# Keeping an input weight by head pairs on 128 rows in an attention-and-MLP kernel

## The chip, the cores and the metric

The kernel runs on one core of a Trainium2 chip. The number that counts is the device time of one execution in microseconds (us), taken as the median of several runs. Times inside an execution come from one profiled execution; its instructions are grouped by source line, and "L399" is line 399 of the kernel as it was before the change.

## What is computed

For each of 8 batches and 8 heads there is a block `x` of 512 tokens by 64 and a block `state` of 32 tokens by 64. Both attend to each other, and the result (512 + 32 tokens, 8 x 64 = 512 wide) goes through a two-layer network with a Mish activation:

```
scores = x @ state.T / 8 ;  xread = softmax(scores) @ state          # (512, 64) per head
scores2 = state @ x.T / 8 ; sread = softmax(scores2) @ x             # (32, 64) per head
y = [xread, sread] with the heads side by side                       # (8 * 544, 512)
h = y @ w_in ; g = h * tanh(log(1 + exp(h))) ; out = g @ w_out       # w_in (512, 2048), w_out (2048, 512)
```

`x` and `state` are 32-bit floats; `w_in` and `w_out` come as 64-bit floats, 8 MB each.

## The kernel before, in words

**The product with the state.** The 512 read tokens of a batch are never formed. Since `xread @ w_in` is softmax times (`state @ w_in`), the kernel first makes the small product `state @ w_in` for a slice of columns (`sw_slice`, PSUM tiles `swp`), splits it into a rounded part and a remainder (`swh`, `swl`), and multiplies that by the transposed softmax (`aT`, split into `ah` and `al`): this is `gemm1`, three products of 128x512 per pair. ScalarE applies Mish (`take_g`), VectorE splits the result (`gh`, `gl`), and `gemm2` multiplies by `w_out`, which is kept in split form too (`wo`).

**Slots.** A slot is one batch `b` and one of eight pieces `j`: 256 of the 2048 columns of `w_in`, that is 12 matmuls of `gemm1` and 24 of `gemm2`. From batch 1 on, one `sw_slice` serves two slots; in batch 0 each slot has its own, half as wide. Four more slots (`gemm1_s`) do the 256 `sread` tokens; before batch 7 they are put in. The slots run one after the other, `gemm2` two slots behind.

**Halves of heads.** Before the change the eight heads are used as two groups, heads 0 to 3 and heads 4 to 7. `w_in_sb` holds 64 rows per head twice: rows 0 to 63 the lower half of the 2048 columns, rows 64 to 127 the upper half, all eight heads beside each other. The state product is 16 matmuls with 64 contraction rows and 32 output rows: for each of two groups, four heads, two halves of the columns. The compiled program issues each as two instructions. For the `sread` slots this layout has to be regrouped: `load_w_s` copies pieces of `w_in_sb` inside SBUF by DMA, 16 transfers of 256 KB.

**Loads.** In batch 0 the weights arrive while the work on them has begun. `load_w_in(e)` brings piece e of `w_in` (called i0 to i7 below) as two transfers, each to 64 rows, in runs of 1 KB; `load_w_out(j)` brings two blocks of 128 rows of `w_out` (o0 to o7) in runs of 4 KB. A raw piece is two 32-bit words per number. ScalarE rescales the high words (`scale_high`, L101) and rounds the low words (`round_low`, L108; for most `w_out` pieces GpSimd does it, L106), and VectorE joins them into a 32-bit float (`join_words`, L119). For `w_out`, VectorE then splits into `wo` (L156, L159). All these loads, and `x`, go through SyncE's queue in the order in which they are written; the first batch's state goes through ScalarE's queue, as three transfers of 32 KB. i0, i1 and i4 to i7 share two buffers, so i4 can start only when i0 is joined. i2 and i3 lie in the places that o6 and o5 take later, and o7 takes the place of the first batch's `x`.

**Order.** Every engine runs its own instructions in order. A scheduler places them; `with behind(...)` in the code says after which earlier instruction something may stand in that order. `fill` issues matmuls whose results nobody uses, between the steps of the first batch.

Of the kernel before, what the change touches and what calls it, by code (L numbers as in the profile page):

```python
# [16 lines left out]
P = 128  # L17
# [22 lines left out]
def state_attention_mish_kernel(ctx, tc, x, state, w_in, w_out, out):  # L40
# [20 lines left out]
    w_in_sb = const.tile([P, H, DF // 2], F32, name="w_in_sb")  # L61
# [6 lines left out]
    def load_x(b):  # L68

        shape = [P, NC, 2, NT * D]  # L70
        if b == 0:
            xs = const.tile(shape, F32, tag="wo7", name="x_0")
        else:
            xs = pool.tile(shape, F32, tag="x", name=f"x_{b}", bufs=1)
        for c in range(NC):
            last["load"] = nc.sync.dma_start(
                xs[:, c], x[b].rearrange("(k c) (p t) d -> c p k (t d)", k=2, t=NT)[c])
        return xs
# [6 lines left out]
    def load_xq(b, xq, parts):  # L85
        for i in parts:
            h, q = divmod(i, 4)
            u, dh = divmod(q, 2)
            nc.sync.dma_start(
                xq[q * 32:(q + 1) * 32, h % NC, h // NC],  # L90
                x[b, h].rearrange("(i w u) d -> u i w d", w=8, u=2)[u][:, :, dh * 32:(dh + 1) * 32])
# [30 lines left out]
    def load_w_in(e):  # L122


        shape, place = [P, H, P, 2], {2: "wo6", 3: "wo5"}.get(e)
        if place:
            raw = const.tile(shape, U32, tag=place, name=f"wir_{e}")
        else:
            raw = pool.tile(shape, U32, tag="raw", name=f"wir_{e}", bufs=2)
        for r in range(2):  # L130
            f0 = 2 * (r * DF // 2 + e * P)
            last["load"] = nc.sync.dma_start(  # L132
                raw[half(r)].rearrange("p c f w -> p c (f w)"),
                w_in[:, f0:f0 + 2 * P].rearrange("(h d) f -> d h f", d=D),
            )
# [63 lines left out]
    def attention(b, xs, sn, xq=None):  # L199
# [97 lines left out]
        def soft1_e():  # L297
# [11 lines left out]
            for kc in two:  # L309
                mx = small["mx"][kc]  # L310
                with behind(*(((0, "sub"),) if b == 0 and kc else ())):
                    nc.vector.tensor_reduce(mx, groups(src[kc]), AX.X, ALU.max)
                last[b, "sub"] = nc.vector.tensor_sub(groups(e1[kc]), groups(src[kc]), wide(mx))
                last[b, "exp"] = nc.scalar.activation(e1[kc], e1[kc], AF.Exp)
# [52 lines left out]
        if b == 0:  # L367
            first = [lambda: (xt(0), xt(1), state_blocks(b, sn), xt(2), xt(3), s_(), soft1_e()),
                     soft1_n, soft1_a]
# [22 lines left out]
    def sw_slice(b, j, n=2 * P):  # L392

        pw = [misc(f"swp_{b}_{j}_{r}") for r in range(2)]
        for kc in range(2):
            for c in range(NC):
                o = slice(c * NS, (c + 1) * NS)
                for r in range(2):
                    last["PE"] = nc.tensor.matmul(  # L399
                        pw[r][o, kc * n:(kc + 1) * n],  # L400
                        bds[b][half(r), kc ^ r, o],
                        w_in_sb[half(r), kc * NC + c, j * P:j * P + n],
                        start=True, stop=True,
                    )
        hi = pool.tile([P, 2, 2, n], F32R, tag="swh", name=f"swh_{b}_{j}")
        lo = pool.tile([P, 2, 2, n], F32R, tag="swl", name=f"swl_{b}_{j}")
        for r in range(2):
            hr = hi[:, r].rearrange("p k f -> p (k f)")
            pr = pw[r][:, :2 * n]
            last["swh"] = nc.scalar.copy(hr, pr)  # L410
            last["swl"] = nc.vector.tensor_sub(lo[:, r].rearrange("p k f -> p (k f)"), pr, as_f32(hr))  # L411
        return {j + i: [t[..., i * P:(i + 1) * P] for t in (hi, lo)] for i in range(n // P)}
# [16 lines left out]
    def gemm1(b, j, aT, sw):  # L429
        swh, swl = sw[j]  # L430
        phs = []
        for k in range(2):
            ph = ps_h.tile([P, 512], F32, tag="ph", name=f"ph_{b}_{j}_{k}")
            seq = []
            for kc in range(2):
                hi, lo = aT[kc]
                seq += [(swh[:, k, kc], hi), (swh[:, k, kc], lo), (swl[:, k, kc], hi)]
# [13 lines left out]

    def load_w_s(j):
        w = pool.tile([P, NC, 2, 2 * P], F32, tag="raw", name=f"ws_{j}", bufs=2)
        f0 = 2 * j * P
        for kc in range(2):
            for r in range(2):
# [4 lines left out]
    def gemm1_s(j, ws):  # L461
# [3 lines left out]
        for r in range(2):  # L465
            for k in range(2):
                w = ws[:, :, r, k * P:(k + 1) * P]
# [17 lines left out]
    def gemm2(key, fcs, gh, gl, ntok, ts=None):  # L485
# [3 lines left out]
        for t in ts or range(ntok):  # L489
            for i, fc in enumerate(fcs):  # L490
# [3 lines left out]
                for n, (g, w) in enumerate(ops):  # L494
                    last["PE"] = nc.tensor.matmul(  # L495
                        accs[key][t], g[:, sl], wo[fc % 8][:, fc // 8, w, :],
# [31 lines left out]
    load(("o", 4), ("i", 6), ("o", 5), ("i", 7), ("o", 6), ("o", 7))  # L528

    first[0]()  # L530
    with behind((0, "exp")):
        scale_words(raws[0])
    new_accs(0, NT)
# [6 lines left out]
    first[1]()  # L540
    with behind("words"):
        scale_high(rawo[0])
    with behind((0, "e1")):
        join_w_in(0, raws.pop(0))
    with behind("PE", "words", "join"):
        first[2]()
    fill(1)
    with behind((0, "ah")):
        round_low(rawo[0])
    with behind("PE", "words", (0, "DVE")):  # L550
        sw_next = sw_slice(0, 0, P)
    fill(2)
    with behind("swh"):
        round_low(raws[1], True)
        scale_high(raws[1])
    ws = {}
    with behind("swl"):
        ws[0] = join_w_out(0, rawo.pop(0))
    with behind("join"):
        join_w_in(1, raws.pop(1))  # L560
# [30 lines left out]
    for n, (key, j) in enumerate(slots):  # L591
        if key == "s":
            if j == 0:
                ws_next = load_w_s(0)
            ws, ws_next = ws_next, load_w_s(j + 1) if j + 1 < 4 else None
            g = gemm1_s(j, ws)
            pending.append((key, (2 * j, 2 * j + 1, 2 * j + 8, 2 * j + 9), g, 2))
# [8 lines left out]
        if (key, j) == (0, 0):  # L606
            with behind("words"):
                g = mish(key, j, phs)
            with behind("PE", "mish"):
                sw_next = sw_slice(0, 1, P)  # L610
# [9 lines left out]
        pending.append((key, (j, j + 8), g, NT))  # L620
        if key == 0 and j + 1 < SLOTS:
# [79 lines left out]
```

## Time and profile before

| | before |
|---|---|
| median of 3 runs | 693.2 us (693.12 to 695.12) |
| profiled execution | 700.21 us, of which 698.4 us from the first to the last instruction |
| TensorE matmul (PE) busy | 682.4 us, 98% |
| VectorE (DVE) / ScalarE (ACT) busy | 342.6 us / 263.6 us |
| mean granted TensorE clock | 0.986 of full speed |
| read from HBM | 32.24 MB, at 219 to 228 GB/s until about 87 us |
| `w_in` transfers | 16 of 512 KB, median 18.4 us from issue to landing |
| `w_out` transfers | 16 of 512 KB, median 13.7 us |

In the views below, a row of the timeline is: start, length, engine, line, operation, what it writes and reads, how many, and in brackets how long the engine sat idle before it and what ended that. A matmul's end is modelled by the profiler; the starts are measured.

### The profile page before, as it was taken

How to read it: one execution, taken by the hardware profiler on the slowest of the kernel's cores; microseconds unless marked ns; L12 is line 12 of the kernel's file. 1: busy time of each engine (PE TensorE's matmuls, PEld its weight loads, DVE VectorE, ACT ScalarE, POOL GpSimd, SP SyncE). 2: the span in 40 equal slices, each digit the busy share in tenths (PEclk: the TensorE clock that was granted, in tenths of full speed). 3: DMA queues.
4: the chain of work that ended last, by engine and by line, in shares of the span. 5: the costliest groups of instructions: out<-in, count | busy, mean ns of one | idle time of the engine just before them, and what ended most of it. 6: DMA issues, size and time to landing. Idle time of an engine off the chain costs nothing.

```text
span 698.4 us, 11183 instructions
## 1 busy us (share of the span) xinstructions
PE 682.4 (98%) x4718; PEld 529.9 (76%) x4718; DVE 342.6 (49%) x520; ACT 263.6 (38%) x416; POOL 10.6 (2%) x14
## 2 busy tenths in 40 slices
PE   7989999999999999999999999999999999999997
PEld 6767677677777777777777777777777788977785
DVE  2876598484338433753357333843374334332221
ACT  2887666362226312451146122631255113222110
POOL 0001200000000000000000000000000000000000
PEclk8989999999999999999999999999999999999999
DMA  9999832410123010312032011334010007001001
GB/s 224 221 219 228 226 49 68 103 22 23 42 68 49 9 61 20 85 25 61 6 82 41 28 34 66 49 69 121 16 46 1 1 1 181 1 0 31 1 1 61
DMA packets 84530, 46.09 MB, mean 66 GB/s; under 512 B 57600, under 2 KB 78080, under 8 KB 84480
## 3 DMA queue, kind: packets, MB, share of 16 engines
q1 hardware_dynamic: 84048, 45.27, 27.4%
q8 instruction: 37, 0.61, 0.4%
q10 hardware_dynamic: 432, 0.10, 0.1%
q14 instruction: 13, 0.11, 0.1%
HBM read 32.24 MB, written 8.91 MB: 59 GB/s over the span
## 4 chain that ended last, share of the span: by engine, by line
PE 91%; DMA 3%; SPq 2%; ACT 2%; DVE 1%; issue 0%; ACTq 0%; DVEq 0%
PE acc L495 52%; PE ph L441 24%; PE swp L399 5%; PE ph_s L473 3%; PE acc_s L495 3%; DMA wor<-in_moe_w_out_dram 2%; PE srp L348 1%; PE sc L230 1%; SPq L132 1%; PE e2p L276 1%; DMA x<-in_x_dram 1%; SPq L146 1%; ACT L416 1%; ACT g L416 0%; DMA out_dram<-o 0%
## 5 line engine op out<-in xcount | busy, mean ns | idle before, releaser
L495 PE MATMUL acc<-wo,gh 128*128 128x512 f32 x1024 | 329.3, 403 | 0.0
L495 PEld LDWEIGHTS acc<-wo,gh 128*128 128x128 f32 x1024 | 190.3, 190 | 55.6 <-issue 12.3
L495 PE MATMUL acc<-wo,gl 128*128 128x512 f32 x512 | 202.5, 397 | 0.0
L416 ACT ACTIVATE g<-ph 128x512 f32<-128x512 f32 x128 | 74.1, 597 | 221.8 <-DVE gl L423 154.6
L421 DVE CAST gh<-g 128x1024 fp32r<-128x1024 f32 x64 | 44.3, 693 | 161.5 <-PE acc L495 145.9
L495 PEld LDWEIGHTS acc<-wo,gl 128*128 128x128 f32 x512 | 97.2, 190 | 23.6 <-DVE swl L411 0.4
L441 PE MATMUL ph<-ah,swh 128*128 128x512 f32 x256 | 84.2, 401 | 1.9 <-ACT swh L410 1.9
L423 DVE TENSOR_TENSOR gl<-g,gh 128x1024 fp32r<-128x1024 f32 x64 | 78.4, 1226 | 4.9
L441 PE MATMUL ph<-al,swh 128*128 128x512 f32 x256 | 79.5, 392 | 0.0
L441 PE MATMUL ph<-ah,swl 128*128 128x512 f32 x256 | 79.0, 392 | 0.2 <-DVE swl L411 0.2
L411 DVE TENSOR_TENSOR swl<-swp,swh 128x512 fp32r<-128x512 f32 (+1 forms) x72 | 42.7, 625 | 54.4 <-ACT swh L410 53.9
L441 PEld LDWEIGHTS ph<-ah,swh 128*128 128x128 f32 x256 | 47.3, 188 | 15.2 <-ACT swh L410 2.9
L441 PEld LDWEIGHTS ph<-ah,swl 128*128 128x128 f32 x256 | 47.8, 188 | 11.1 <-DVE swl L411 0.6
L441 PEld LDWEIGHTS ph<-al,swh 128*128 128x128 f32 x256 | 48.1, 188 | 10.7
L399 PE MATMUL swp<-w_in_sb,bd 64*32 64x256 f32 (+1 forms) x1152 | 41.1, 364 | 3.8 <-DVE w_in_sb L119 3.7
L410 ACT CAST swh<-swp 128x512 fp32r<-128x512 f32 (+1 forms) x72 | 35.6, 546 | 18.2 <-PE swp L399 18.2
L416 ACT ACT_TABLE_LOAD x21 | 26.9, 1283 | 28.0 <-PE e2p L276 11.3
L399 PEld LDWEIGHTS swp<-w_in_sb,bd 64*32 64x32 f32 x1152 | 18.8, 108 | 21.8 <-issue 14.3
L504 ACT COPY o<-acc 128x512 f32<-128x512 f32 x16 | 9.4, 587 | 44.9 <-PE acc L495 25.1
L470 DVE TENSOR_TENSOR wl<-ws,wh 128x512 fp32r<-128x512 f32 x16 | 11.1, 691 | 27.3 <-PE ph_s L473 23.3
L208 DVE STREAM_TRANSPOSE xT<-xq 128x512 f32<-128x512 f32 x24 | 24.2, 1087 | 0.3 <-PE e2p L276 0.3
L502 DVE COPY o<-acc 128x512 f32<-128x512 f32 x16 | 11.0, 690 | 22.4 <-DMA out_dram<-o 16.4
(83 smaller groups left out, 523.7 us busy)
## 6 DMA issues: line engine op xcount, KB each, us to landing
x<-in_x_dram SPq DMA_DIRECT2D x32, 256.0 KB, 4.2
wir<-in_moe_w_in_dram SPq DMA_DIRECT2D x16, 512.0 KB, 18.4
wor<-in_moe_w_out_dram SPq DMA_DIRECT2D x16, 512.0 KB, 13.7
out_dram<-o SPq DMA_DIRECT2D x32, 256.0 KB, 2.3
xq<-in_x_dram SPq DMA_DIRECT2D x192, 32.0 KB, 2.3
ws<-w_in_sb SPq DMA_DIRECT2D x16, 256.0 KB, 4.7
sn<-in_state_dram SPq DMA_DIRECT2D x21, 32.0 KB, 1.8
out_dram<-o_s SPq DMA_DIRECT2D x8, 64.0 KB, 1.7
```

The lines of the kernel that those rows point to most:

```text
L208: nc.vector.transpose(xTs[c].rearrange("p (k v i g) -> p g k v i", k=2, v=2, g=4), xq[:, c].rearrange("p k (g v) d -> p g k v d", v=2))
L399: last["PE"] = nc.tensor.matmul(pw[r][o, kc * n:(kc + 1) * n], bds[b][half(r), kc ^ r, o], w_in_sb[half(r), kc * NC + c, j * P:j * P + n], ...
L410: last["swh"] = nc.scalar.copy(hr, pr)
L411: last["swl"] = nc.vector.tensor_sub(lo[:, r].rearrange("p k f -> p (k f)"), pr, as_f32(hr))
L416: last["mish"] = nc.scalar.activation(g[:, k * 512:(k + 1) * 512], ph, AF.Mish)
L421: nc.vector.tensor_copy(gh, g)
L423: last["gl"] = nc.vector.tensor_sub(gl, g, as_f32(gh))
L441: last["PE"] = nc.tensor.matmul(ph, l, r, start=(i == 0), stop=(i == len(seq) - 1))
L470: nc.vector.tensor_sub(lo, w, as_f32(hi))
L473: nc.tensor.matmul(ph[r][:, k * 256:(k + 1) * 256], l[:, c], srT[i][:, c], start=(c == 0 and n == 0), stop=(c == NC - 1 and n == 2))
L495: last["PE"] = nc.tensor.matmul(accs[key][t], g[:, sl], wo[fc % 8][:, fc // 8, w, :], start=(fc == 0 and n == 0), stop=(fc == NFC - 1 and ...
L502: nc.vector.tensor_copy(o, accs[key][t])
```

## The change

The heads are now used as even and odd ones. `w_in_sb` holds 128 rows of `w_in` (two neighbouring heads) on 128 partitions, four pairs beside each other, with all 2048 columns in their natural order. A piece of `w_in` is loaded as two transfers of two pairs each, to all 128 rows, in runs of 2 KB. The state product becomes 8 matmuls: for each of four pairs, the even head on rows 0 to 63 and the odd one on rows 64 to 127, each over twice as many columns (512; 256 in batch 0). The `sread` slots read `w_in_sb` as it is, and `load_w_s` is gone. `x` and `state` are put in the new order when they are loaded; for the state this gives the source four blocks of 32 rows with gaps between them, where it was 128 rows on end. Piece j of `w_out` is now the blocks 2j and 2j+1, not j and j+8. In batch 0 the words of i0 and i1 are rescaled earlier, those of o0 later, and the last loads stand in another order.

```
-    w_in_sb = const.tile([P, H, DF // 2], F32, name="w_in_sb")
+    w_in_sb = const.tile([P, NC, DF], F32, name="w_in_sb")
...
     def load_w_in(e):
-        shape, place = [P, H, P, 2], {2: "wo6", 3: "wo5"}.get(e)
+        shape, place = [P, NC, 2 * P, 2], {2: "wo6", 3: "wo5"}.get(e)
...
-        for r in range(2):
-            f0 = 2 * (r * DF // 2 + e * P)
+        w = w_in.rearrange("(c p) f -> p c f", p=P)[..., 4 * e * P:4 * (e + 1) * P]
+        for c in range(0, NC, 2):
             last["load"] = nc.sync.dma_start(
-                raw[half(r)].rearrange("p c f w -> p c (f w)"),
-                w_in[:, f0:f0 + 2 * P].rearrange("(h d) f -> d h f", d=D),
-            )
+                raw[:, c:c + 2].rearrange("p c f w -> p c (f w)"), w[:, c:c + 2])
...
     def load_state(b):
             (nc.sync if b else nc.scalar).dma_start(
-                sn[:, i, :], state[b].rearrange("(a c) n d -> a (c n) d", a=2)[i % 2])
+                sn[:, i, :], state[b].rearrange("(c a) n d -> a c n d", a=2)[i % 2])
...
-    def sw_slice(b, j, n=2 * P):
-        pw = [misc(f"swp_{b}_{j}_{r}") for r in range(2)]
+    def sw_slice(b, j, n=2):
+        f = slice(j * 2 * P, (j + n) * 2 * P)
+        pw = [misc(f"swp_{b}_{j}_{kc}")[:, :n * 2 * P] for kc in range(2)]
+        for c in range(NC):
+            o = slice(c * NS, (c + 1) * NS)
+            for kc in range(2):
+                last["PE"] = nc.tensor.matmul(
+                    pw[kc][o, :], bds[b][half(kc), 0, o], w_in_sb[half(kc), c, f], start=True, stop=True)
...
-    def load_w_s(j):
-        w = pool.tile([P, NC, 2, 2 * P], F32, tag="raw", name=f"ws_{j}", bufs=2)
-        f0 = 2 * j * P
-        for kc in range(2):
-            for r in range(2):
-                nc.sync.dma_start(
-                    w[half(kc), :, r], w_in_sb[half(r), kc * NC:(kc + 1) * NC, f0:f0 + 2 * P])
-        return w
...
-    load(("o", 4), ("i", 6), ("o", 5), ("i", 7), ("o", 6), ("o", 7))
+    load(("o", 4), ("o", 6), ("o", 5), ("i", 6), ("i", 7), ("o", 7))
...
-    with behind((0, "exp")):
+    with behind((0, "scs")):
         scale_words(raws[0])
...
+    with behind((0, "exp")):
+        scale_words(raws[1])
...
+    with behind("swh", "join"):
+        scale_words(rawo[0])
         ws[0] = join_w_out(0, rawo.pop(0))
```

Three places in the compiled order. The first is ScalarE in batch 0, from the first exponentials (L314, `e`) to the first Mish. The tiles `wir_96` and `wir_102` are i0 and i1, `wor_99` is o0, and `wir_105` is i2. Before:

```order
L314 ACTIVATE e_0_0_207<-e_0_0_207 128x512
L314 ACTIVATE e_0_1_208<-e_0_1_208 128x512
L101 ACTIVATE wir_96<-wir_96 128x1024
L108 ACTIVATE wir_96<-wir_96 128x1024
L101 ACTIVATE wor_99<-wor_99 128x1024
L334 CAST ah_0_272<-at_0_267 128x512
L334 CAST ah_1_281<-at_1_276 128x512
L108 ACTIVATE wor_99<-wor_99 128x1024
L410 CAST swh_0_306<-swp_0_0_288 128x256
L410 CAST swh_0_306<-swp_0_1_289 128x256
L101 ACTIVATE wir_102<-wir_102 128x1024
L416 ACT_TABLE_LOAD
```

And now:

```order
L101 ACTIVATE wir_96<-wir_96 128x1024
L108 ACTIVATE wir_96<-wir_96 128x1024
L313 ACTIVATE e_0_0_209<-e_0_0_209 128x512
L313 ACTIVATE e_0_1_210<-e_0_1_210 128x512
L101 ACTIVATE wir_102<-wir_102 128x1024
L108 ACTIVATE wir_102<-wir_102 128x1024
L333 CAST ah_0_273<-at_0_268 128x512
L333 CAST ah_1_282<-at_1_277 128x512
L403 CAST swh_0_298<-swp_0_0_288 128x256
L403 CAST swh_0_298<-swp_0_1_289 128x256
L101 ACTIVATE wor_99<-wor_99 128x1024
L108 ACTIVATE wor_99<-wor_99 128x1024
```

Both words of i0 now stand before the exponentials and both of i1 before `ah`; the words of o0 have moved behind `swh`.

The second place is SyncE's queue after the load of the second batch's `x` (`x_126`). Before, `wir_138` and `wir_144` were i6 and i7, and `wor_135`, `wor_141`, `wor_147`, `wor_150` were o4 to o7:

```order
L76 DMA x_126<-in_x_dram 128x2x256 x4
L165 DMA sn_131<-in_state_dram 128x64 x3
L146 DMA wor_135<-in_moe_w_out_dram 128x1024 x2
L165 DMA sn_1143<-in_state_dram 128x64 x3
L132 DMA wir_138<-in_moe_w_in_dram 64x8x256 x2
L146 DMA wor_141<-in_moe_w_out_dram 128x1024 x2
L132 DMA wir_144<-in_moe_w_in_dram 64x8x256 x2
L146 DMA wor_147<-in_moe_w_out_dram 128x1024 x2
```

Now `wor_138` is o6, `wor_141` is o5, and `wir_144` and `wir_147` are i6 and i7:

```order
L76 DMA x_126<-in_x_dram 128x2x256 x4
L163 DMA sn_131<-in_state_dram 128x1x64 x3
L144 DMA wor_135<-in_moe_w_out_dram 128x1024 x2
L163 DMA sn_1071<-in_state_dram 128x1x64 x3
L144 DMA wor_138<-in_moe_w_out_dram 128x1024 x2
L144 DMA wor_141<-in_moe_w_out_dram 128x1024 x2
L132 DMA wir_144<-in_moe_w_in_dram 128x2x512 x2
L132 DMA wir_147<-in_moe_w_in_dram 128x2x512 x2
```

The two `w_out` pieces stand ahead of the two `w_in` pieces; a transfer of `w_in` has 128 rows with two runs of 512 words, where it had 64 rows with eight runs of 256.

The third place is TensorE around the state product of slot 4 in batch 0. Before:

```order
L441 MATMUL ph_3_1_575<-ah_1_281,swl_3_511 128x512
L399 MATMUL swp_4_0_585<-w_in_sb,bd_167 32x128 x8
L399 MATMUL swp_4_1_586<-w_in_sb,bd_167 32x128 x8
L495 MATMUL acc_0_233<-wo_449,gh_2_516 128x512 x2
L495 MATMUL acc_0_233<-wo_449,gl_2_517 128x512
```

And now:

```order
L435 MATMUL ph_3_1_543<-ah_1_282,swl_3_479 128x512
L398 MATMUL swp_4_0_553<-w_in_sb,bd_167 32x256 x4
L398 MATMUL swp_4_1_554<-w_in_sb,bd_167 32x256 x4
L480 MATMUL acc_0_233<-wo_425,gh_2_484 128x512 x2
L480 MATMUL acc_0_233<-wo_425,gl_2_485 128x512
```

The slice stands at the same place; it has half as many matmuls, each over twice the columns.

More of the change, by code (lines that the diff above doesn't have):

```diff
@@ L313, in soft1_e @@
                 last[b, "sub"] = nc.vector.tensor_sub(groups(e1[kc]), groups(src[kc]), wide(mx))
-                last[b, "exp"] = nc.scalar.activation(e1[kc], e1[kc], AF.Exp)
+                with behind(*(("words",) if b == 0 else ())):
+                    last[b, "exp"] = nc.scalar.activation(e1[kc], e1[kc], AF.Exp)
         def soft1_n():
@@ L367, in attention @@
         if b == 0:
-            first = [lambda: (xt(0), xt(1), state_blocks(b, sn), xt(2), xt(3), s_(), soft1_e()),
-                     soft1_n, soft1_a]
+            first = [lambda: (xt(0), xt(1), state_blocks(b, sn), xt(2), xt(3), s_()),
+                     soft1_e, soft1_n, soft1_a]
             fills.append(fill)
@@ L389, in attention @@
         return [], pieces, aT
-    def sw_slice(b, j, n=2 * P):
-        pw = [misc(f"swp_{b}_{j}_{r}") for r in range(2)]
-        for kc in range(2):
-            for c in range(NC):
-                o = slice(c * NS, (c + 1) * NS)
-                for r in range(2):
[L399 to L412, printed above, removed]
+    def sw_slice(b, j, n=2):
[6 more added lines that the diff above has]
+                    pw[kc][o, :], bds[b][half(kc), 0, o], w_in_sb[half(kc), c, f], start=True, stop=True)
+        hi = pool.tile([P, 2, n * 2 * P], F32R, tag="swh", name=f"swh_{b}_{j}")
+        lo = pool.tile([P, 2, n * 2 * P], F32R, tag="swl", name=f"swl_{b}_{j}")
+        for kc in range(2):
+            last["swh"] = nc.scalar.copy(hi[:, kc], pw[kc])
+            last["swl"] = nc.vector.tensor_sub(lo[:, kc], pw[kc], as_f32(hi[:, kc]))
+        return {j + i: [t[:, :, i * 2 * P:(i + 1) * 2 * P] for t in (hi, lo)] for i in range(n)}
     def take_g(g, k, ph):
@@ L436, in gemm1 @@
                 hi, lo = aT[kc]
-                seq += [(swh[:, k, kc], hi), (swh[:, k, kc], lo), (swl[:, k, kc], hi)]
+                h, l = (t[:, kc, k * P:(k + 1) * P] for t in (swh, swl))
+                seq += [(h, hi), (h, lo), (l, hi)]
             seq = seq[::3] + seq[1::3] + seq[2::3]
@@ L449, in mish, with gemm1_s @@
         return g
-    def load_w_s(j):
-        w = pool.tile([P, NC, 2, 2 * P], F32, tag="raw", name=f"ws_{j}", bufs=2)
-        f0 = 2 * j * P
-        for kc in range(2):
-            for r in range(2):
-                nc.sync.dma_start(
-                    w[half(kc), :, r], w_in_sb[half(r), kc * NC:(kc + 1) * NC, f0:f0 + 2 * P])
-        return w
-    def gemm1_s(j, ws):
+    def gemm1_s(j):
         g = new_g(f"s_{j}")
@@ L466, in gemm1_s @@
             for k in range(2):
-                w = ws[:, :, r, k * P:(k + 1) * P]
+                fc = 4 * j + 2 * r + k
+                w = w_in_sb[:, :, fc * P:(fc + 1) * P]
                 hi, lo = (pool.tile([P, NC, P], F32R, tag="t", name=f"w{n}_{j}_{r}_{k}", bufs=5) for n in "hl")
@@ L539, in state_attention_mish_kernel @@
     fill(0)
-    first[1]()
-    with behind("words"):
-        scale_high(rawo[0])
+    first[2]()
+    with behind((0, "exp")):
+        scale_words(raws[1])
     with behind((0, "e1")):
@@ L545, in state_attention_mish_kernel @@
     with behind("PE", "words", "join"):
-        first[2]()
+        first[3]()
     fill(1)
[L548 to L551, printed above, removed]
+    with behind("PE", (0, "ah"), (0, "DVE")):
+        sw_next = sw_slice(0, 0, 1)
     fill(2)
-    with behind("swh"):
-        round_low(raws[1], True)
-        scale_high(raws[1])
     ws = {}
     with behind("swl"):
+        join_w_in(1, raws.pop(1))
+    with behind("swh", "join"):
+        scale_words(rawo[0])
         ws[0] = join_w_out(0, rawo.pop(0))
-    with behind("join"):
-        join_w_in(1, raws.pop(1))
     with behind("join"):
@@ L592, in state_attention_mish_kernel @@
         if key == "s":
[L593 to L597, printed above, removed]
+            g = gemm1_s(j)
+            pending.append((key, range(4 * j, 4 * j + 4), g, 2))
             second()
@@ L609, in state_attention_mish_kernel @@
             with behind("PE", "mish"):
-                sw_next = sw_slice(0, 1, P)
+                sw_next = sw_slice(0, 1, 1)
             fill(3)
```

17 lines of the change are left out of this document (9 added, 8 removed).

## The prediction

> **What bounds the kernel now.** The first view is the page: the busy shares, then the slices with the granted clock and the traffic.
>
> ```profile
> PE 682.4 (98%) x4718; PEld 529.9 (76%) x4718; DVE 342.6 (49%) x520; ACT 263.6 (38%) x416; POOL 10.6 (2%) x14
> PEclk8989999999999999999999999999999999999999
> GB/s 224 221 219 228 226 49 68 103 22 23 42 68 49 9 61 20 85 25 61 6 82 41 28 34 66 49 69 121 16 46 1 1 1 181 1 0 31 1 1 61
> ```
>
> TensorE is busy 98%, yet the clock falls only in early slices, and only the first five slices carry steady traffic. So the second view is the busy time of each engine by stage (stretch, its length, the engines, clock, DMA share, GB/s).
>
> ```profile
> 0.00:20.00 20.00, 16.07 (x108) 13.29 (x109) 7.56 (x15) 6.06 (x8) 0.70 (x6) 0.83 0.97 224
> 20.00:75.00 55.00, 49.08 (x438) 37.13 (x437) 39.50 (x56) 42.78 (x58) 6.17 (x5) 0.91 1.03 225
> 125.00:560.00 435.00, 435.00 (x3048) 333.02 (x3047) 213.90 (x337) 153.91 (x255) 0.00 (x0) 1.00 0.18 44
> 560.00:640.00 80.00, 80.00 (x459) 67.04 (x458) 29.18 (x38) 19.41 (x35) 0.00 (x0) 1.00 0.19 47
> ```
>
> From 125 us on TensorE works without a pause at full clock: there only fewer or shorter matmuls count. From 20 to 75 us it stands idle for 6 us and loses clock, while the DMA engines are full: there the loads can count. The third view, the chain of waits, has both kinds.
>
> ```profile
> 1.73 6.35 DMA x<-in_x_dram
> 19.67 14.63 DMA wor<-in_moe_w_out_dram
> 45.74 8.14 PE acc L495 x24
> 161.00 1.02 PE swp L399 x32
> 162.03 5.78 PE acc L495 x24
> ```
>
> A `w_out` load stands on the chain for 14.63 us; the same 24 matmuls of `gemm2` take 8.14 us behind it and 5.78 us later.
>
> **The loads of `w_in`.** Four stretches of 2 us (columns as above) tell what the DMA engines reach: with `x` alone (128 rows, runs of 1 KB), with `w_in` (64 rows, runs of 1 KB), with `w_in` and `w_out` mixed, and with `w_out` alone (128 rows, 4 KB).
>
> ```profile
> 4.00:6.00 2.00, 2.00 (x11) 2.00 (x10) 0.00 (x0) 0.39 (x1) 0.00 (x0) 1.00 0.97 309
> 28.00:30.00 2.00, 2.00 (x43) 1.71 (x38) 1.97 (x3) 1.28 (x3) 0.00 (x0) 1.00 1.11 189
> 46.00:48.00 2.00, 2.00 (x6) 1.52 (x6) 1.71 (x6) 1.98 (x5) 0.00 (x0) 0.50 1.01 224
> 80.00:82.00 2.00, 2.00 (x12) 1.62 (x12) 0.11 (x1) 1.86 (x2) 0.00 (x0) 1.00 1.03 412
> ```
>
> Runs of 1 KB reach 309 GB/s, so the 189 of `w_in` is not the run length. It is the 64 rows, which the change does away with, or the reading of short runs from far-apart rows of `w_in`, which it only doubles in length. The new rate lies between 189 and 412; I take 309, the nearest row with 128 rows. By the Trainium skill ("DMA: Bandwidth & Descriptors", section "Where 436 GB/s comes from") the 16 ports into SBUF are the limit at 435 GB/s; half the rows would then have half of it, an estimate of 218, with which the 189 above and the 225 of the whole stretch agree.
>
> What late loads cost is in the waits from 20 to 75 us (in total, times, longest) and in the timeline.
>
> ```profile
> ACT wor L101 <- DMA wor<-in_moe_w_out_dram: 5.7, 4, 2.5
> ACT L101 <- DMA wir<-in_moe_w_in_dram: 1.2, 1, 1.2
> ```
>
> ```profile
> 27.86 0.67 PE L399 MATMUL swp<-w_in_sb,bd 64*32 64x128 f32 x32 [1.08 <-DVE w_in_sb L119]
> 34.32 1.19 ACT L101 ACTIVATE wor<-wor 128x1024 f32<-128x1024 f32 x1 [1.49 <-DMA wor<-in_moe_w_out_dram]
> 36.82 1.09 ACT L416 ACTIVATE g<-ph 128x512 f32<-128x512 f32 x2
> 43.26 1.22 DVE L119 SCALAR_TENSOR_TENSOR w_in_sb<-wir 128x1024 uint32<-128x1024 uint32 x1
> 44.63 1.11 PE L399 MATMUL swp<-w_in_sb,bd 64*32 64x128 f32 x32 [2.63 <-DVE w_in_sb L119]
> 65.15 1.14 ACT L101 ACTIVATE wor<-wor 128x1024 f32<-128x1024 f32 x1 [2.50 <-DMA wor<-in_moe_w_out_dram]
> 67.51 1.28 ACT L416 ACT_TABLE_LOAD   x1 [1.22 <-PE ph L441]
> 68.65 0.33 PE L360 MATMUL srTp<-ident,srd 128*128 128x128 f32 x1 [0.76 <-DVE srd L356]
> ```
>
> ScalarE waits 5.7 + 1.2 us for loads, but that is not the gain. First, the wait of 1.49 us for o1 at 34.32 delays Mish of slot 1 (36.82), behind which VectorE splits and only then joins i3 (43.26), for which TensorE waits 2.63 us. Without it all of this moves up by 1.5 us, and by 0.6 more through ScalarE's new order (next part): **-2.1 us** at 44.63. The waits for i3, o2 and o3 behind it then vanish too, but by then VectorE's queue and TensorE itself set the pace: 0. Second, the idle 2.63 us was followed by half clock (0.50 in the row from 46 to 48) and the 8.14 us above, 2.4 more than 5.78. About 1.7 us of idle will be left: the join moves up 2.1, the matmuls before it some 1.2 (0.6 through ScalarE's order and as much from waits inside them, an estimate). Behind the 1.08 us at 27.86 the clock stayed at 1.00 (row from 28 to 30), behind the 2.63 it did not; halfway, **-1.2**, bounds 0 and -2.4. Third, of the 2.50 us for o4, ScalarE would have waited until 67.51 for TensorE anyway; what is late is a join in VectorE's queue and the 0.76 us before L360: **-0.8**. Together -4.1, bounds 0 and -5.3. What is late next is ScalarE's own chain: two table loads of 1.28 us, three rescalings and Mish in every slot.
>
> **ScalarE's order before the first `gemm1`.** Today:
>
> ```profile
> 20.23 1.20 ACT L101 ACTIVATE wor<-wor 128x1024 f32<-128x1024 f32 x1
> 21.29 1.07 ACT L334 CAST ah<-at 128x512 fp32r<-128x512 f32 x2
> 22.23 1.20 ACT L108 ACTIVATE wor<-wor 128x1024 uint32<-128x1024 uint32 x1
> 22.03 0.67 PE L399 MATMUL swp<-w_in_sb,bd 64*32 64x128 f32 x32
> 23.30 0.64 ACT L410 CAST swh<-swp 128x256 fp32r<-128x256 f32 x2
> 23.73 0.74 PE L441 MATMUL ph<-ah,swh 128*128 128x512 f32 x2 [0.39 <-ACT swh L410]
> 24.29 1.14 ACT L101 ACTIVATE wir<-wir 128x1024 f32<-128x1024 f32 x1 [0.34 <-DMA wir<-in_moe_w_in_dram]
> ```
>
> The second o0 step, 1.20 us, leaves the place before `swh`; `ah` still has to wait for its transposes. `swh` then follows L399 at 22.7 and not 23.3: -0.6, counted above. The i0 and i1 steps that now stand earlier lie in ScalarE's waits for the softmax, if i1 has landed by about 18.6 us (21.29, less some 0.4 that `ah` may start sooner, less two steps of 1.14). `x`, i0, o0 and i1 are 4.2 MB; from 1.73 on, when `x` first moves, and with 2 us until a transfer has landed (the median of the small state loads, next part) they have 14.9 us: 282 GB/s. At 309 it is hidden; below 282, `ah` waits and the first `gemm1` with it.
>
> **The head and the state load.** The whole softmax chain starts with the state and `x`. The rows are the page's queue that the first state load has to itself, the landing times of all state loads, and two waits.
>
> ```profile
> q10 hardware_dynamic: 432, 0.10, 0.1%
> DMA to landing us min/median/max: 1.7/2.0/5.9
> 7.72 0.33 PE L174 MATMUL st<-ident,sn 128*128 128x128 f32 x1 [1.03 <-DMA sn<-in_state_dram]
> 9.47 0.64 PE L214 MATMUL xTp<-ident,x 128*128 128x128 f32 x4 [0.63 <-DMA x<-in_x_dram]
> ```
>
> The last `x` waits until 9.47 although 1 MB at 309 GB/s is over 3.4 us after the first byte: i0 runs beside it. With i0 no longer on half the rows this can give up to -1.5 us. Against that, the first state load (5.9 us to landing, later ones 2.0) reads four blocks now. If the blocks, not the rows, are dealt out to the engines, four of them carry 96 runs each instead of 24. A run is some 26 ns (0.1% of 16 x 698.4 us over 432), a run of `x` beside it 53 ns (1 KB at 309/16 GB/s): 96 x 79 = 7.6 us against 1.9, so +5.7. Nothing here shows which, and the bytes and rows are the same as today; between -1.5 and +5.7 I take **+1.0**, nearer to the transfer that the trace has.
>
> **The state product.** Twice the columns at half the count is the same streaming. Whether the count itself costs shows in batch 0, where slot 5 has half of the instructions by themselves:
>
> ```profile
> 35.10 0.67 PE L399 MATMUL swp<-w_in_sb,bd 64*32 64x128 f32 x32
> 68.91 0.64 PE L399 MATMUL swp<-w_in_sb,bd 64*32 64x128 f32 x16
> ```
>
> These 16 pass the array four at a time in four rounds, the 32 eight at a time in four rounds; 16 instructions more cost 0.03 us. The new slice has 16 fewer and two rounds of double length: 36 slices by 0.03 is -1.1, the bound; the other is 0, **-0.3** taken. Since both groups must be evacuated before a second product of `gemm1`, up to 0.3 us a slot comes back where TensorE waits for `swh`, in batch 0 alone; it is within the bounds.
>
> **The regrouping copies** go: 0, since TensorE is busy 80.00 of 80.00 us there. SyncE's new order at the end: 0, since the waits of ScalarE for o1 to o4 are all it has for `w_out` today, and o4 keeps its place; o5 to o7, i6 and i7 have slack.
>
> **Sum.** -4.1 + 1.0 - 0.3 = -3.4 us. The profiled execution took 700.21 us (698.4 plus 1.8 around it), 7.0 over the median, and part of these 7 may be the load stage; the terms are differences, taken off 693.2: **689.8 us**.
>
> **Rivals.**
> 1. The state comes late: -4.1 - 0.3 + 5.7, less 0.8 for waits for `x` that it covers, is +0.5: 693.7. If two thirds of its runs stand beside the new 2 KB runs of `w_in` (106 ns), it is 32 x 79 + 64 x 132 = 11.0 us, +9.1 instead of +5.7, and 697.1. For it speaks the new shape, against it that bytes and rows are unchanged. The Trainium skill ("DMA: Bandwidth & Descriptors", section "Why a DMA increments its semaphore by 16 and not by 1") says that a transfer is dealt over the largest number up to 16 that divides the slowest dimension on both sides; by that rule this load, with 4 on the source side, gets four engines and the rival holds. No run here shows such a load.
> 2. Slower: `w_in` stays near 200 GB/s because of its far-apart source rows. Then i1 lands at 24.3 as today (ScalarE starts on it at 24.29), its two steps of 1.14 us now stand before `ah`, and `ah` starts at 26.6 instead of 21.29. Of these 5.3 us the loads, which run on meanwhile, give back most of the later waits (1.49 + 1.2): +2.6, 695.8. It decides as soon as the first 4.2 MB run below 282 GB/s. Against it: 309 and 412 on 128 rows.
> 3. It does nothing: without the profiler the load stage has little to wait for, and the rest cancels: 693.
>
> **How the numbers follow.** A measurement of this kernel tells 0.3% (2.1 us) from no change. The forecast has 0.46 (faster 0.43, same 0.03), with its own range of 685.5 (-5.3 - 1.5 - 1.1, rounded) to 691.5; rival 1 has 0.28 (same 0.14, slower 0.12, faster 0.02), rival 2 0.14 (slower 0.13, same 0.01), rival 3 0.12 (same 0.09, faster 0.03). Faster 0.48, same 0.27, slower 0.25. The range, 685.5 to 696.0, leaves out the far end of rivals 1 and 2.
>
> **What would show it.** Right: over 280 GB/s between 6 and 40 us, no wait of L101 for a load, the first 128x512 matmul before 24 us, `sw_slice` in batch 1 and later at 1.00 to 1.02 us, and equal times from 125 us on but for a shift. Wrong: the state's transpose (now L172) after 10 us is rival 1; ScalarE waiting for i1 before `ah` is rival 2; a shorter `sw_slice` means that instruction count did cost.

## The result and the profile after

The changed kernel takes **699.83 us** (median of 11 runs, 694.41 to 702.37), the kernel before 693.75 us (11 runs, 692.13 to 696.28). The ratio is **1.0083**, with a 95% interval of 1.0058 to 1.0108: slower by 5.8 us (4.0 to 7.5). The prediction said 689.8 us and faster, with a range of 685.5 to 696.0.

The profiled execution of the changed kernel took 697.67 us. It is faster than the one shown of before (700.21), although the kernel is slower. So a second profile of the kernel before was taken (run e1 below); that execution took 691.30 us, and in what follows "before" means this one. Both profiled executions lie some 2 us under the medians of their kernels, so they can be compared. Granted clock and traffic in 40 slices of before, then the page of the changed kernel: busy shares, the same slices, and the queue of the first state load.

```profile
PEclk9999999999999999999999999999999999999999
GB/s 241 253 244 272 144 32 141 51 0 62 7 85 39 25 40 69 49 11 62 7 96 27 63 0 77 54 55 123 31 32 1 1 16 169 1 4 28 1 1 61
```

```profile
PE 680.2 (98%) x4142; PEld 516.8 (74%) x4142; DVE 344.9 (50%) x520; ACT 262.0 (38%) x415; POOL 12.6 (2%) x13
PEclk7999999999999999999999999999999999999999
GB/s 316 360 248 182 34 34 101 78 10 57 10 73 50 1 61 37 74 18 61 7 86 37 58 4 71 48 6 61 30 31 1 1 1 61 0 9 23 0 1 60
q10 hardware_dynamic: 396, 0.10, 0.1%
```

The loads did become faster: the first slices carry 316 and 360 GB/s instead of 241 and 253. But the clock is low in the first slice, and the state's queue has 396 packets instead of 432. The three transfers have 384 rows of 256 bytes between them; 48 packets are over before, 12 now, that is 16 and 4 for each transfer. In the traces these extra packets have 4 bytes each. The state's packets lie between 2.16 and 5.49 us before and between 2.77 and 9.37 us now.

Busy time by stretch (its length, the engines, granted clock, DMA share, GB/s), first of before, then of the changed kernel.

```profile
6.00:40.00 34.00, 28.85 (x270) 22.38 (x269) 28.67 (x41) 25.63 (x36) 3.69 (x3) 1.00 1.09 250
10.00:17.00 7.00, 5.96 (x52) 5.80 (x52) 6.09 (x13) 3.99 (x6) 0.00 (x0) 1.00 1.07 278
```

```profile
6.00:40.00 34.00, 29.41 (x212) 22.52 (x211) 23.74 (x35) 22.44 (x31) 5.26 (x3) 0.85 0.99 358
10.00:17.00 7.00, 6.24 (x48) 4.11 (x49) 2.10 (x4) 2.68 (x4) 0.00 (x0) 0.50 1.04 400
```

TensorE runs at half clock from 10 to 17 us, and VectorE gets 2.10 us of work done there instead of 6.09: the whole chain is later. TensorE's timeline says why: before, then changed (start, length, instruction, in brackets the idle time ahead of it and what ended it).

```profile
5.74 0.65 PE L174 MATMUL st<-ident,sn 128*128 128x128 f32 x2
7.96 1.95 PE L230 MATMUL sc<-xT,bd 64*32 64x256 f32 x32
10.67 1.12 PE L295 MATMUL scT<-ident,scs 128*128 128x128 f32 x8 [0.75 <-ACT scs L243]
20.30 0.73 PE L441 MATMUL ph<-ah,swh 128*128 128x512 f32 x2 [0.34 <-ACT swh L410]
```

```profile
7.28 0.30 PE L172 MATMUL st<-ident,sn 128*128 128x128 f32 x1 [1.07 <-DMA sn<-in_state_dram]
9.88 0.47 PE L172 MATMUL st<-ident,sn 128*128 128x128 f32 x1 [2.29 <-DMA sn<-in_state_dram]
11.99 2.81 PE L228 MATMUL sc<-xT,bd 64*32 64x256 f32 x32
15.56 1.97 PE L293 MATMUL scT<-ident,scs 128*128 128x128 f32 x8 [0.76 <-ACT scs L241]
25.82 0.96 PE L435 MATMUL ph<-ah,swh 128*128 128x512 f32 x3
```

The second transpose of the state waits 2.29 us for its load and starts at 9.88. Behind this wait the scores take 2.81 us instead of 1.95 and their transposes 1.97 instead of 1.12. The first `gemm1` starts at 25.82 instead of 20.30.

### The profile page after: what moved, and what is told of

Its sections match the earlier page's. It is cut to its first block, busy times and chain, and to the rows that moved or that the text cites. A ratio compares the mean times of both kernels' runs of the same rounds, so it can differ in the third digit from the quotient of the medians.

```text
span 695.9 us, 10040 instructions
## 1 busy us (share of the span) xinstructions
PE 680.2 (98%) x4142; PEld 516.8 (74%) x4142; DVE 344.9 (50%) x520; ACT 262.0 (38%) x415; POOL 12.6 (2%) x13
## 4 chain that ended last, share of the span: by engine, by line
PE 93%; ACT 4%; DMA 1%; issue 1%; ACTq 0%; DVE 0%
PE acc L480 51%; PE ph L435 24%; PE swp L398 5%; PE ph_s L458 3%; PE acc_s L480 3%; PE sc L228 2%; PE srp L347 1%; DMA sn<-in_state_dram 1%; PE e2p L274 1%; PE acc L246 1%; ACT L409 1%; ACT wor L101 1%; ACT g L409 1%; PE xTp L212 0%; ACT L101 0%
## 5 line engine op out<-in xcount | busy, mean ns | idle before, releaser
L398 PE MATMUL swp<-w_in_sb,bd 64*32 64x512 f32 (+1 forms) x576 | 41.6, 554 | 1.9 <-DVE sm L261 1.8
L455 DVE TENSOR_TENSOR wl<-w_in_sb,wh 128x512 fp32r<-128x512 f32 x16 | 11.1, 692 | 29.1 <-PE ph_s L458 25.1
L306 DVE STREAM_TRANSPOSE e<-scs 128x512 f32<-128x512 f32 x14 | 9.1, 691 | 24.1 <-ACT scs L241 24.1
```

Of the source, the lines that this page charges most:

```text
L398: last["PE"] = nc.tensor.matmul(pw[kc][o, :], bds[b][half(kc), 0, o], w_in_sb[half(kc), c, f], start=True, stop=True)
L455: nc.vector.tensor_sub(lo, w, as_f32(hi))
```

## The experiments

Each ratio is to runs of the kernel before on the same chip; 0.1% is 0.7 us. Where heads are exchanged or a step is left out, it is said.

**e1, e2: both kernels again, unchanged.**

> The kernel before, unchanged: a second profile of it, and the spread of its times. The profile shown with the prediction took 700.21 us, 7 us over the median of its timed runs. Theory A (that profile was an unusual execution): this profile is near 694, with its load stage some 5 us shorter than in the first, and the ratio is 1.000. Theory B (the profile is typical and only the timing differs): the profile is near 700 again.

> The changed kernel, unchanged: a second profile, and whether its times keep their spread (694.4 to 702.4). Theory state-late (the state load of batch 0, which reads four blocks, lands late, by an amount that differs from execution to execution): ratio 1.008 again, and the second transpose of the state starts at 9.9 us or later. Theory load-and-order (the loads of w_in or ScalarE's new order cost it): ratio 1.008 again, but the state's transposes no later than in the first profile while the loss shows after 15 us.

e1: 1.0009 (0.9979 to 1.0038), profile 691.30 us. Theory A held: the profile that the prediction used was an unusual execution of the kernel before, with half clock in the head and the first `gemm1` at 23.73 instead of 20.30. Its mean clock was 0.986; the 33 timed executions of before beside e1 have 0.990 to 1.000. e2: 1.0086 (1.0050 to 1.0122), second transpose at 10.92: the late state is there again.

**e3: the changed kernel, state in one block** (heads 0 to 3 stand for 0, 2, 4, 6; the work is the same).

```diff
-state[b].rearrange("(c a) n d -> a c n d", a=2)[i % 2]
+state[b].rearrange("(a c) n d -> a (c n) d", a=2)[i % 2]
```

> The changed kernel with the state read as before, 128 rows in one block (heads 0 to 3 for heads 0, 2, 4, 6, so the state product is of other heads; the work is the same). Theory state-late: the second transpose of the state starts by 8 us instead of 9.9, and the ratio to the kernel before falls from 1.008 to between 0.994 and 1.000. Theory load-and-order: the ratio stays at 1.008, within 0.003.

1.0023 (0.9995 to 1.0051); the transposes start at 5.92, the first `gemm1` at 19.69, the clock is 1.00 from 10 to 17. Against 1.0083 the state load is worth **0.60%, 4.2 us**. The ratio did not fall below 1: something else takes what the loads give.

**e4: the kernel before with the changed kernel's state load alone** (other heads, the same work), the diff of e3 turned round.

> The kernel before with the changed kernel's state load alone (four blocks of 32 rows; other heads than the reference, the same work). Theory state-late: ratio 1.005 to 1.012, the state's second transpose at 10 us or later. Theory load-and-order: ratio 1.000, within 0.003.

1.0081 (1.0041 to 1.0121): **+5.6 us** from this line alone. The queue and TensorE's timeline:

```profile
q10 hardware_dynamic: 396, 0.10, 0.1%
7.29 0.30 PE L174 MATMUL st<-ident,sn 128*128 128x128 f32 x1 [1.89 <-DMA sn<-in_state_dram]
8.33 0.48 PE L174 MATMUL st<-ident,sn 128*128 128x128 f32 x1 [0.73 <-DMA sn<-in_state_dram]
10.44 2.81 PE L230 MATMUL sc<-xT,bd 64*32 64x256 f32 x32
```

The same 396 packets, a wait, and half clock behind it. The second transpose came earlier (8.33) than the expected 10 us.

**e5: the changed kernel, state by head pairs** (the heads as in the change).

```diff
+if b == 0:
+    for c in range(NC):
+        nc.scalar.dma_start(sn[c * NS:(c + 1) * NS, 0:2, :],
+                            state[b, 2 * c:2 * c + 2].rearrange("a n d -> n a d"))
+    nc.vector.tensor_copy(sn[:, 2, :], sn[:, 0, :])
+    return sn
```

> The changed kernel with the right heads, but the state of batch 0 loaded in four transfers, one for each head pair (32 rows, both heads at a time), and the third copy made by VectorE instead of a third load. Theory state-late (a load whose source has four blocks is carried by four engines): each of the four loads is spread over 16 engines again, the second transpose of the state starts by 8 us, no half clock in the head, and the ratio to the kernel before is 1.002 as with the state in one block (0.999 to 1.005). Rival (the far-apart rows of the source cost it, not the sharing out): these rows are as far apart as in the change, so the ratio stays at 1.008.

1.0015 (0.9991 to 1.0039). The rows lie as far apart as in the change, so distance is not the cause; e3, with all 384 rows, shows that their number is not. There are 256 rows and 64 packets over, 16 for each of the four transfers:

```profile
q10 hardware_dynamic: 320, 0.07, 0.0%
6.67 0.56 PE L178 MATMUL st<-ident,sn 128*128 128x128 f32 x2 [0.25 <-DMA sn<-in_state_dram]
20.38 0.96 PE L441 MATMUL ph<-ah,swh 128*128 128x512 f32 x3
```

By these counts a source that starts with a dimension of 32 (or 128) is shared out over 16, one that starts with 4 over four. That is the rule of the Trainium skill ("DMA: Bandwidth & Descriptors", section "Why a DMA increments its semaphore by 16 and not by 1"), which the prediction gave to its first rival; the counts and the times agree with it.

**e6: matmuls in the wait.** The changed kernel with 6 and 12 matmuls on the identity ahead of the state's two transposes (the accumulators that they write are set up earlier for it).

```diff
 for s in range(2):
+    if b == 0:
+        with behind("xt"):
+            for _ in range((6, 12)[s]):
+                nc.tensor.matmul(accs[0][NT - 1][:, :P], ident, ident, ...)
```

> The changed kernel with 18 more matmuls on the identity (some 4 us) put between the transposes of x and those of the state, so that TensorE does not idle while the state is late. Theory clock (the wait itself is some 3 us and the half clock that follows it another 3 us): the granted clock stays at 1.00 from 10 to 17 us and the ratio falls from 1.008 to about 1.004. Theory wait-alone (the late state costs all 6 us, the clock nothing): the ratio stays at 1.008, or rises by what the added matmuls delay.

1.0048 (1.0026 to 1.0070). TensorE's timeline and the stretch as above:

```profile
10.50 0.27 PE L176 MATMUL st<-ident,sn 128*128 128x128 f32 x1
11.88 1.94 PE L232 MATMUL sc<-xT,bd 64*32 64x256 f32 x32
14.58 1.12 PE L297 MATMUL scT<-ident,scs 128*128 128x128 f32 x8 [0.75 <-ACT scs L245]
10.00:17.00 7.00, 6.17 (x69) 4.75 (x69) 3.47 (x6) 3.50 (x5) 0.00 (x0) 1.00 1.04 393
```

The second transpose is no earlier than in the change (10.50 against 9.88), but scores and transposes take 1.94 and 1.12 us, and the first `gemm1` starts at 23.73 instead of 25.82. Over its 12 timed executions the mean clock is 0.997, in the change 0.992. So of the late state's 4.2 us some 2.4 (0.35%, with intervals of 0.2 to 0.25% on both ratios) are the half clock that follows the wait, the rest the wait. The split is rough: the added matmuls end only at the second transpose and may themselves delay it a little.

**e7: slow loads.** e3 with each slice of `w_in` in two transfers of 64 rows.

```diff
-for c in range(0, NC, 2):
-    ... raw[:, c:c + 2] ..., w[:, c:c + 2]
+for r in range(2):
+    ... raw[half(r)] ..., w[half(r)]
```

> As the run with the state in one block (ratio 1.0023), but each slice of w_in comes in two transfers of 64 rows each, as before the change, instead of two of 128 rows; the runs of 2 KB stay (other heads than the reference, the same work). Theory hidden (w_in's rate is hidden behind ScalarE and VectorE, which are busy for 9.9 and 10.0 of the 10 us from 35 to 45): the rate falls to some 220 to 250 GB/s between 6 and 35 us and the ratio stays at 1.002 to 1.004. Theory worth-4-us (the prediction's first term): the ratio rises to 1.008.

1.0090 (1.0051 to 1.0130), 255 GB/s from 6 to 40 us where e3 has 379. The theory "hidden" fell: in the change's orders the rate is worth 0.67%, 4.6 us. ScalarE and TensorE:

```profile
21.16 1.10 ACT L101 ACTIVATE wir<-wir 128x1024 f32<-128x1024 f32 x1 [5.37 <-DMA wir<-in_moe_w_in_dram]
```

```profile
24.53 1.65 PE L435 MATMUL ph<-ah,swh 128*128 128x512 f32 x3 [3.38 <-ACT swh L403]
```

ScalarE waits 5.37 us for i1 in front of `ah`: the prediction's second rival, which the change only escapes because its loads are fast (in e3 ScalarE waits 0.6 us for `w_in`).

**e9, e10, e13, e14: the orders.** e3 (fast loads) and e7 (slow loads), with ScalarE's and VectorE's order at the start of batch 0 as before the change (e9, e10), and with SyncE's order at the end of the loads as before too (e14, e13). The first lines of ScalarE's order, and SyncE's:

```diff
-    with behind((0, "scs")):
+    with behind((0, "exp")):
         scale_words(raws[0])
...
-load(("o", 4), ("o", 6), ("o", 5), ("i", 6), ("i", 7), ("o", 7))
+load(("o", 4), ("i", 6), ("o", 5), ("i", 7), ("o", 6), ("o", 7))
```

> As the run with the state in one block (fast loads of w_in, ratio 1.0023), with ScalarE's and VectorE's order at the start of batch 0 as before the change (the exponentials first, the words of i1 after the first swh). Theory order-needs-rate (the new order costs nothing while w_in is fast, 5 us when it is slow): ratio 1.002, within 0.003. Theory order-is-the-gain: the ratio rises by what the new order saves, some 0.001 to 0.002 (the first gemm1 then starts at 20.5 instead of 19.73). Theory order-costs: it falls to 0.996, below the kernel before.

> As the run with the state in one block and w_in in halves of 64 rows (slow loads, ratio 1.009, with 5.37 us of ScalarE waiting for i1 in front of ah), with ScalarE's and VectorE's order as before the change. Theory order-needs-rate: the wait for i1 moves behind the first gemm1, the first gemm1 starts at about 21 instead of 24.6 and the ratio falls to 1.002 to 1.004: in the old order the rate of w_in is worth almost nothing. Theory rate-is-worth-4-us: the ratio stays at 1.006 or more in either order.

> As the run with slow loads (halves of 64 rows) and ScalarE's old order (ratio 1.0062), with SyncE's order at the end of the loads as before the change too (o4, i6, o5, i7, o6, o7). Theory tail-order (with slow loads the new end order lets i6 land 3.65 us too late, and a half clock follows): that wait and the half clock after it go, and the ratio falls to 1.001 to 1.003. Theory rate-only: the ratio stays at 1.006.

> The same two old orders with the fast loads of the change (128 rows), state in one block. Theory gain-spent-on-orders (before's orders already hide slow loads): ratio 1.001 to 1.002, the same as the run before it within 0.002, so that in before's orders the rate of w_in is worth nothing that can be measured. Theory rate-worth: 0.003 or more below the run before it.

| orders | slow loads | fast loads | the rate is worth |
|---|---|---|---|
| both new | 1.0090 (e7) | 1.0023 (e3) | 0.67% |
| ScalarE's old | 1.0062 (1.0033 to 1.0091) (e10) | 1.0017 (0.9995 to 1.0039) (e9) | 0.45% |
| both old | 1.0035 (1.0007 to 1.0064) (e13) | 0.9995 (0.9966 to 1.0024) (e14) | 0.40% |

With slow loads each new order costs some 0.27%, which is within the intervals; with fast loads neither costs or saves anything that can be told. In e10 the wait for i1 in front of `ah` is gone and the first `gemm1` starts at 20.71 instead of 24.53, yet the ratio fell less than expected. There i6 is late, which now stands behind two more pieces of `w_out`:

```profile
69.57 1.28 ACT L101 ACT_TABLE_LOAD   x1 [3.65 <-DMA wir<-in_moe_w_in_dram]
```

In e13 ScalarE's longest wait for `w_in` is 0.7 us. The rate is worth something in every row, so the theory that before's orders leave the rate without value is not borne out; with intervals of about 0.3% on each ratio the 0.40% (2.8 us) is not certain either.

**e8, e15: whole products.** The scheduler puts a state product's 8 matmuls where it finds room, and in the change it cuts products that stood in one piece. e8 is e5 with the products of batches 1 and 2 told to follow the `gemm1` in front of them.

```diff
 if nb < B and nj % 2 == 0:
-    sw_next = sw_slice(nb, nj)
+    with behind(*(("PE",) if key < 2 else ())):
+        sw_next = sw_slice(nb, nj)
```

> As the run with the state in four transfers by head pair, and the state products of batches 1 and 2 told to stand behind the gemm1 in front of them, so that the one at slot 4 of batch 1 is no longer cut in two by 12 matmuls of gemm1. Theory cut: a product costs about 1.0 us however few of its matmuls run together, so its two pieces (0.97 and 1.01 us) become one of 1.0 and the time falls by 1 us, ratio 0.0014 below that of the state by head pairs. Theory no-cut: the pieces hide behind other work and the ratio is the same within 0.0005 in the profile's marks.

1.0011 (0.9992 to 1.0030). One product of batch 1 on TensorE: before, changed, e8 (the trace has two records for each matmul).

```profile
133.31 1.09 PE L399 MATMUL swp<-w_in_sb,bd 64*32 64x256 f32 x32
```

```profile
135.32 1.04 PE L398 MATMUL swp<-w_in_sb,bd 64*32 64x512 f32 x2
139.22 1.08 PE L398 MATMUL swp<-w_in_sb,bd 64*32 64x512 f32 x14
```

```profile
134.86 1.09 PE L404 MATMUL swp<-w_in_sb,bd 64*32 64x512 f32 x16
```

One matmul takes 1.04 us, eight take 1.09: here a piece costs about the same however few it holds, and the cut cost 1.0 us. The time itself moved by less than its interval; this verdict rests on the rows. A second place lies around the four "s" slots of the last batch. There the change's pieces take 3.16 us from 565 to 625, those of before 2.54. e15 makes them whole too, upon e12 (next).

```diff
-("PE",) if key < 2 else ()
+("PE",) if key < 2 or key == B - 1 else ()
```

> The version with the state by head pairs, whole slices in batch 1 and the late exponentials (ratio 1.000), with the state product of slot 2 of the last batch whole as well. Theory cut: 0.44 us less in the profile from the 1920th to the 2016th product of gemm1 and gemm2, ratio 0.999 to 1.000. Theory no-cut: no difference.

Time in `swp` from 565 to 625 us, of e12, then of e15 (all engines that touch the tile; the first is TensorE):

```profile
565.00:625.00 60.00, 3.16 (x16) 0.44 (x16) 1.38 (x2) 1.07 (x2) 1.00 0.08 25
```

```profile
565.00:625.00 60.00, 1.09 (x16) 0.18 (x16) 1.29 (x2) 1.08 (x2) 1.00 0.09 27
```

Three pieces became one, 2.07 us less where TensorE never pauses; the 0.44 expected had one of the pieces in view. e15 takes **690.32 us, 0.9940 (0.9917 to 0.9964): faster than both kernels.** Its ratio is 0.6% below e12's; the rows account for 0.3%, the rest lies inside the two intervals.

**e11, e12: what TensorE waits for in the load stage.** e11 is e5 and leaves out ScalarE's rescaling of the high words of o1 to o7. e12 is e8 with the exponentials of the second softmax moved from slot 2 to slot 3, and the step behind them with it.

```diff
-scale_words(rawo[o], True)
+round_low(rawo[o], True)
```

```diff
-elif j == 1:
+elif j == 2:
     with behind("words"):
         rest[1]()
...
-for _ in range((0, 0, 1, 1)[j] if key == 0 and j < 4 else 1 + (key == 0)):
+for _ in range((0, 0, 0, 2)[j] if key == 0 and j < 4 else 1 + (key == 0)):
```

> The changed kernel with the state in four transfers by head pair, less ScalarE's step on the high words of o1 to o7 (the L101 step of wor; 7 steps of about 1.15 us; the weights come out wrong, everything else stays). Theory ScalarE-bound (with fast loads ScalarE's own work sets the pace from 24 to 45 us, 9.9 of 10 us busy): TensorE's wait for the product of slot 3 (2.9 us) falls below 1 us, and the ratio falls from 1.0015 to 0.996 or less. Theory load-bound: the waits stay, now ended by a load, and the ratio stays within 0.002.

> The version with the state by head pairs and whole slices (ratio 1.0011), with the exponentials of batch 0's second softmax (1.9 us of ScalarE) moved from slot 2 to slot 3, behind TensorE's wait for the product of slot 3. Theory ScalarE-bound: that wait (2.7 us and at times a half clock after it) shrinks by 1.5 to 2 us; if the 1.9 us aren't missed again in slot 4, the time falls by that, ratio 0.998 to 0.999; if they are, it stays at 1.001.

e11: 0.9980 (0.9956 to 1.0004); e12: 1.0000 (0.9980 to 1.0019). TensorE's wait for the product of slot 3, before, e5, e11 and e12:

```profile
40.08 0.67 PE L399 MATMUL swp<-w_in_sb,bd 64*32 64x128 f32 x32 [2.55 <-DVE w_in_sb L119]
```

```profile
39.69 0.67 PE L404 MATMUL swp<-w_in_sb,bd 64*32 64x256 f32 x16 [1.88 <-DVE sm L267]
```

```profile
38.88 0.67 PE L404 MATMUL swp<-w_in_sb,bd 64*32 64x256 f32 x16 [1.00 <-DVE sm L267]
```

```profile
39.69 0.67 PE L404 MATMUL swp<-w_in_sb,bd 64*32 64x256 f32 x16 [2.07 <-DVE w_in_sb L119]
```

With fast loads it is 1.88 in e5, 2.21 in e8 and 2.39 in e3, so little shorter than 2.55. In this stage both helpers are full (as above, from 35 to 45 us; before, e5, e11):

```profile
35.00:45.00 10.00, 7.45 (x63) 5.72 (x62) 9.58 (x16) 9.93 (x15) 1.43 (x1) 1.00 1.08 244
```

```profile
35.00:45.00 10.00, 8.12 (x43) 5.95 (x42) 9.40 (x16) 9.94 (x15) 1.11 (x1) 0.83 0.98 330
```

```profile
35.00:45.00 10.00, 9.00 (x53) 6.78 (x52) 9.93 (x15) 9.16 (x14) 1.13 (x1) 1.00 0.90 306
```

ScalarE is busy 9.93 of 10 us before and 9.94 in e5. Taking seven of its steps away, some 7 us, gave 0.35% (2.4 us) and left VectorE with 9.93; the ratio of 0.996 or less that was expected did not come. "ScalarE-bound" is half of it: behind ScalarE stands VectorE. Moving the exponentials (e12) left this wait about as it was (2.07 us, 2.21 in e8); the expected 1.5 us were not found there.

## Why the prediction was wrong

**The ladder**, each step from two ratios above, in us at 693.75: the new layout with slow loads, before's orders and an early state, +2.4 (e13); fast loads, -2.8 (e14 against e13); the change's orders, +1.9 (e3 against e14, not distinct from 0); the late state, +4.2 (the change against e3). Sum +5.7, against 5.8 measured; the last step is clearly outside its uncertainty, the first only just (0.5 to 4.4), the two between are not.

The forecast of -3.4 was 9.1 us off this sum: 3.2 at the head (+1.0 against +4.2), 3.2 at the loads with the orders (-4.1 against -0.9, which is known to some 3 us only) and 2.7 at the state product (-0.3 against +2.4). The head alone does not explain the miss: with 4.2 in its place the sum would have been 693.0, still inside the range. Without the late state, e3 is 1.6 us slower than before (-0.3 to +3.5), where the other terms of the prediction give -4.4.

- **The head's +1.0 is the step that failed and that the runs settle.** The prediction saw the four blocks, priced four engines at +5.7, and then took a value "nearer to the transfer that the trace has". That transfer had another shape, so its row said nothing for the new one. Rival 1's mechanism is what happened; its +5.7 stands against 5.6 (e4) and 4.2 (e3). That the price fits so well is luck: from its first packet to its last the load took only 3.3 us more (6.6 instead of 3.3), and by e6 the larger part of what it cost is not the transfer but the half clock that the wait brings on. The prediction named the half clock behind idle time, but only at slot 3.
- **The loads, -4.1, failed as well:** as a worth of the rate the size was right (2.8 to 4.6, the 2.8 uncertain), and 309 GB/s was too careful (358 in the mean, 400 from 10 to 17 us). As a step from before to after it was too large. Its largest part rested on the 2.63 us wait for i3's join at 44.63; with fast loads the wait is still there (1.77 in the change, 1.88 in e5), ended by other work of VectorE. "What is late next is ScalarE's own chain" was written and priced only for the waits behind it.
- **The base.** Waits were priced in an execution of 700.21 us. In that of 691.30, ScalarE's largest wait for a `w_in` load up to 45 us is 0.94 us, and the clock is 1.00 through the whole load stage, so the -1.2 for half clock had nothing to win there. The prediction noted the 7 us and took the terms as differences all the same.
- **The state product, -0.3:** whole products take the same before and after (1.09 us, and 0.67 in batch 0): by these rows count costs nothing. No term had the cuts, +1.0 in batch 1 and +0.6 at the "s" slots, though the order of the changed kernel's instructions has them. This is 1.6 of the ladder's +2.4; the other 0.8 stays open.
- **The copies, 0, and steady work:** right. From 125 to 555 us TensorE is busy 430.00 of 430.00 us before and after.
- **SyncE's order, 0:** with the loads of the change no cost can be told from it, as forecast; with those of e10 it costs ScalarE a wait of 3.65 us for i6. Rival 2's wait for i1 is real (e7, 5.37 us) but needs slow loads. Rival 3, no difference, is out.
- Of what was to show it, the rate (358 GB/s), ScalarE without a wait for a load, and 1.02 us for the products that stay whole came true. The first 128x512 matmul came after 24 us, and `st` at 9.88, just under the 10 us set for rival 1. The times are not equal but for a shift from 125 us on: the cut product lies at 135.

## What to carry to other kernels

When a rearrangement gives a transfer's source a short outer dimension, price it by how many engines can share it, and count the queue's packets beyond its rows to see how many did. Give a load at the head of the program its own shape even if it costs more issues: here some 2.4 of its 4.2 us were the half clock behind the wait. Before pricing waits from one profile, ask how far that execution lies from the median, and price a faster load by what still ends the wait when the load is early.

## What the runs showed of the hardware

The same 96 KB of state, in the same number of rows, cost 4.2 to 5.6 us more for the order of its dimensions alone. Rows of `w_in` that lie far apart in memory did not slow its load: in stretches where its packets alone were under way it ran at 404 GB/s with runs of 2 KB on 128 rows (the change, 12 to 14 us), and at 222 with the same runs on 64 rows at a time (e7, 18 to 20 us). It was the 64 rows.

Half clock does not follow every wait of this length: behind the 2.55 us at slot 3 before, the clock stayed at 1.00, behind 1.88 in e5 it was 0.83 in the mean from 35 to 45 us. The traces record when the granted clock changed: in each of them the changes lie on a grid of 3.41 us (in e5 down at 40.70 and up at 44.11, in the change down at 9.27 and up at 19.51, three steps later). The wait of e5 lies within one step of its grid (37.29 to 40.70); that of before is split over two, 1.01 and 1.54 us. In all traces of this case, up to 58 us, a step at full clock in which TensorE stood idle for 1.8 us or more was followed by half clock, and one with less was not. Later steps lost the clock behind less (1.06 us in e7 at 79 us), so this is not the whole rule, and no run was made to test it.

The grid lies differently in each execution, and the times differ with the clock: the twelve of e14 go from 692.45 us at a mean clock of 1.000 to 697.71 at 0.992.

VectorE and GpSimd delayed each other in e3, and each time it was the later one that took longer. GpSimd's step takes 1.11 us when it starts at 21.82, and VectorE's join behind it 1.97 instead of 1.22. At 27.15 VectorE's `gl` starts first; the step of GpSimd then takes 2.19, and the join at 28.46, while that step still runs, 1.97 again (VectorE, then GpSimd).

```profile
22.02 1.97 DVE L119 SCALAR_TENSOR_TENSOR w<-wor 128x1024 uint32<-128x1024 uint32 x1 [0.46 <-ACT wor L108]
27.15 1.22 DVE L416 TENSOR_TENSOR gl<-g,gh 128x1024 fp32r<-128x1024 f32 x1
28.46 1.97 DVE L119 SCALAR_TENSOR_TENSOR w_in_sb<-wir 128x1024 uint32<-128x1024 uint32 x1
30.35 1.22 DVE L119 SCALAR_TENSOR_TENSOR w<-wor 128x1024 uint32<-128x1024 uint32 x1
```

```profile
21.82 1.11 POOL L106 TENSOR_SCALAR wor<-wor 128x1024 uint32<-128x1024 uint32 x1 [20.51 <-DMA wor<-in_moe_w_out_dram]
27.16 2.19 POOL L106 TENSOR_SCALAR wor<-wor 128x1024 uint32<-128x1024 uint32 x1 [4.23 <-DMA wor<-in_moe_w_out_dram]
```
